# Another order for the opening of a gated linear attention and squared-ReLU kernel: the steps, loads, weight pieces and zero products of the first four blocks, and two copies on another engine

## The chip, the core and the metric

The kernel runs on one core of a Trainium2 chip. The core has a matrix engine (TensorE; PE in the profile, its weight loads PEld), three elementwise engines (VectorE or DVE, ScalarE or ACT, GpSimd or POOL), a queue from which the transfers of this kernel are issued (SyncE, SP), and 16 DMA engines that carry them out. The metric is the device time of one execution in microseconds, lower is better. Times of the old kernel: 517.73, 518.93 and 519.45 us, median 518.93.

## What is computed

Two parts follow each other. The first is a recurrence over 768 time steps for 4 batches and 8 heads of 48 channels, with a decay `alpha` for each channel; its output, turned to 3072 tokens of 384 channels, goes through two dense layers with a squared ReLU between them.

```python
# q, k, v, alpha: (4, 8, 768, 48), float32
for t in range(S):
    state = alpha[:, :, t, :, None] * state + einsum('bhd,bhe->bhde', k[:, :, t], v[:, :, t])
    y[:, :, t] = einsum('bhd,bhde->bhe', q[:, :, t], state)
x = y.transpose(0, 2, 1, 3).reshape(3072, 384)
h = maximum(x @ w_in, 0.0)          # w_in (384, 2048)
out = (h * h) @ w_out               # w_out (2048, 384)
```

The two weight matrices come to the kernel as 64-bit floats, the rest as 32-bit ones.

## The kernel before

**Tiling.** The recurrence is cut into 24 blocks, one for each batch and each stretch of 128 time steps; block n belongs to batch n % 4. Blocks 0 to 3 are the first stretch of each batch and make up the first group of 512 tokens. The dense layers work on such groups: the first layer has 16 slices of 128 hidden channels, j = 0 to 15. The weights come in 16 pieces, 8 of `w_in` and 8 of `w_out`; a piece of `w_in` serves two slices (piece 0 for j = 0 and 1, piece 1 for j = 2 and 3).

**The opening.** Everything up to the first four slices of the first group is written out by hand as a string of words, `AT['first']`. A word is the name of a step and its block (or slice, or piece). A loop reads the string from left to right and emits the instructions of each step; every engine, and the DMA queue too, gets its instructions in exactly this order. What follows (slices 4 to 15 of the first group, then groups 1 to 5) is merged from lists with due times by a planner that the change does not touch.

The words, for a block n, with the engine and the line of the profile:

- `load` (SP, L109): one transfer of 192 KB, of `a` (alpha), `q`, `k` or `v`. The string `AT['pre']` gives six loads that are issued ahead of `first`: two blocks' a, q and k. `weights` (SP, L109): a transfer of 767 KB, the next piece of weights; the number behind the word is not used, pieces come in their own order. `move` lets a transfer wait for an earlier one: it walks back over the transfers before it, adding up their assumed lengths (1.1 for a load, 2.3 for a piece), and waits for the first at which the sum has reached 2.25.
- `ln` (ScalarE, L261): logarithm of alpha. `cs` (TensorE, L283): its running sum over the 128 steps, by a product with a triangle of ones, in two passes. `ei`, `eb` (ScalarE, L298 and L294): exp of the sum with minus and plus sign. `mk`, `mq` (VectorE, L302): k and q times these.
- `qT`, `kT` (TensorE, L354): q or k turned, four transposes into one PSUM bank. `qc`, `kc` (L368): the copy of that bank into SBUF, by ScalarE or VectorE according to `AT['cp']`.
- `lt` (TensorE L337, ScalarE L344): the last row of exp, turned, and two copies of it. `sc` (TensorE, L413): scores k by q. `kv` (TensorE, L442): sums k by v, into the same two banks. `am` (VectorE, L424): masked scores. `us` (VectorE, L456), `st` (VectorE, L477 and L479): the state at the half and at the end of the block.
- `ya`, `yb` (TensorE, L393): the output y of two blocks n and n+1, in two banks, with a GpSimd instruction (L518) between the two parts. `ep` (L616): one of four parts of the copies of y into the tiles `x`; twelve copies for two blocks, each by VectorE if (n, bank, part) is in `AT['evd']`, else by ScalarE.
- `first` (ScalarE, L179) and `second` (VectorE, L192 to L199): a piece of weights made into 32-bit floats, two instructions on ScalarE, then four on VectorE.
- `ha`, `hb` (TensorE, L919; ScalarE, L925 and L928): slice j of the first layer for tokens 0 to 255 (`ha`, x of blocks 0 and 1) or 256 to 511 (`hb`, blocks 2 and 3), six products in three thirds of 128 channels each; then ReLU and square.
- `warm` (TensorE, L237) and `zeros` (TensorE, L381): products of a tile of zeros whose results nobody reads; `zeros4` stands for four products, each of which shows as two matmuls. Three `warm` products are issued ahead of the string.

What is moved and who copies is decided in two places:

```python
copy = nc.vector.tensor_copy if f"{x}{n}" in AT["cp"] else nc.scalar.copy          # copied, L368
copy = nc.vector.tensor_copy if (n, e, p) in AT["evd"] else nc.scalar.copy         # ev, L616
```

The names that the first lookup asks for are those of a letter and a block, such as 'q2'. The old list holds 'q2a', 'k2b' and the like.

Of the kernel before, what the change touches and what calls it, by code (L numbers as in the profile page):

```python
# [18 lines left out]


GB = 4
AT = {'thrp': 4.5, 'cvo': 3.35, 'thr': 2.25, 'm48': 16, 'cvs': 3.9, 'cv1': 0.125, 'later': (0, 0, 4, 6, 0, 1, 0), 'evs': 0.1, 'lead': 4, 'post': 3, 'w_first': (46.0, 38.0, 49.0), 'wstep': 1.0, 'w_in_at': 2.5, 'w_in_by': 3.6, 'room1': 22, 'room': 24, 's0': 4, 'ahead': 6, 'late': 2, 'xs': 0.0, 'g0': ((0.5, 4, False, True, 27.75), (25.75, 6, True, True), (29.25, 8, True, False)), 'sc0': (3.25, 2.35, 2.35), 'g1': ((5.5, 8, False, 15.0), (13.0, 10, True), (35.25, 12, True)), 'g': ((2.075, 6, True), (14.25, 8, True)), 'g1x': 51.0, 'gx': 48.75, 'g0x': 56.25, 'k0': 2, 'h0': 15, 'k1': 4, 'h1': 3, 'h1by': 2, 'evs0': 0.7, 'tp': 'ADMD', 'tp1': 'ADAD', 'split': 8, 'o0': (46.5, 48.5), 'o1': (), 'o2': (21.25, 24.75, 24.5, 40.0, 35.25, 28.25), 'str1': 21.5, 'ga': 9.75, 'gb': 12.5, 'cv0': -1.25, 'pre': '1a 0a 0q 0k 1k 1q', 'cp': ('q2a', 'k2b', 'k0a', 'k3a', 'k3b', 'k0b', 'q0b', 'q3b', 'q2b', 'q3a'), 'evd': ((0, 0, 0), (0, 0, 1), (0, 1, 2), (0, 1, 3), (2, 0, 3), (2, 1, 1), (2, 1, 2)), 'first': 'ln0 load1v cs0 ei0 eb0 zeros4 mk0 mq0 qT0 kT0 ln1 cs1 kc0 ei1 warm0 load0v eb1 mk1 qc0 weights0 lt1 sc0 load2a mq1 load2q kT1 kc1 qT1 load2k load3a qc1 load3k kv0 am0 first0 load3v sc1 ln2 kv1 load3q us0 am1 weights6 us1 cs2 ya0 ei2 second0 eb2 lt0 ln3 yb0 load2v mq2 qT2 mk2 load4a ep00 ep01 qc2 kT2 cs3 kc2 eb3 ei3 zeros1 sc2 ep02 mq3 mk3 kT3 ep03 weights2 first1 st0 ha0 second1 lt2 kv2 am2 qT3 load4k kc3 qc3 ha1 weights5 first2 sc3 kv3 am3 load4q us2 ha2 us3 ya2 yb2 weights3 ep20 ep21 ep22 load4v ep23 second2 first3 weights1 st1 weights4 ha3 lt3 hb0 st2 second3 hb2 hb3 hb1 st3'}


RUN = {0: 128, 32: 32, 64: 64, 96: 32}
# [3 lines left out]
def kernel(  # L29
# [78 lines left out]
    def move(us, out, in_):  # L108
        ins = nc.sync.dma_start(out=out, in_=in_).ins  # L109
        ahead = 0.0  # L110
        for before, took in reversed(under_way):
            if ahead >= AT["thrp" if us == 1.0 else "thr"]:
                tc.add_manual_dep(
# [16 lines left out]
    def load(n, xs="aqkv"):  # L130
        c, b = divmod(n, B)
        for x in xs:
            t = tile_of(x, n)
            if id(t) in owner:
                need(("free", *owner[id(t)]))
            owner[id(t)] = x, n
            given.add((x, n))
            move(
                1.1,
                out=t[:, :, 0:D] if x in "qk" else t.rearrange("a (h d) -> a h d", h=H),  # L140
                in_=srcs[x][b, :, c * C : (c + 1) * C, :].rearrange("h s d -> s h d"),
            )
# [57 lines left out]

    for word in AT["pre"].split():
        load(int(word[0]), word[1:])
# [52 lines left out]
    def work(name, bufs=1):  # L255
        return p2.tile([128, NP, C], FP32, tag=name, name=name, bufs=bufs)
# [7 lines left out]

    SPLIT = AT["split"]

# [98 lines left out]
    def copied(x, n):  # L365
        t = blk[n][f"{x}s"] = work(f"{x}s", 2 if x == "k" else 4)
        copy = nc.vector.tensor_copy if f"{x}{n}" in AT["cp"] else nc.scalar.copy
        copy(out=t, in_=blk[n].pop(f"{x}T"))  # L368
# [64 lines left out]
    def state_sums(n):  # L433
        need(("v", n), ("kb", n))
        given.add(("free", "k", n))
        ps = two[n]
        m = D if n >= AT["m48"] else 64
        for p in range(NP):
# [25 lines left out]
    def rows_of(n):  # L464
        return [slice(0, D), slice(64, 64 + D)] if n >= AT["m48"] else [slice(0, 128)]

# [712 lines left out]
```

## Time and profile before

| what | value |
|---|---|
| median of three runs | 518.93 us (517.73 to 519.45) |
| span of the profiled execution | 518.6 us |
| TensorE busy | 507.8 us, 98% |
| VectorE, ScalarE, GpSimd busy | 355.7 us, 306.4 us, 5.3 us |
| DMA, mean over the span | 197 GB/s, 102.34 MB |
| first 5 us: TensorE busy | 2.93 us |
| 15 to 20 us: TensorE, VectorE, ScalarE busy | 3.90, 4.67, 3.30 us |
| 20 to 25 us: TensorE, VectorE, ScalarE busy | 3.64, 4.83, 4.47 us |
| 40 to 60 us: TensorE busy | 20 of 20 us |

The span runs from the first to the last instruction of one execution. An engine's busy time is the sum of the times in which it carries out instructions; TensorE's ends are modelled, since its products overlap. The opening is the first 41 us or so; the stretches in the table show where in it TensorE stands still.

### The profile page before, as it was taken

To read this page: it belongs to the slowest core of one execution; us is meant where nothing else is said; L and a number is where in the kernel's file an instruction comes from. 1 tells how busy PE (TensorE), PEld (TensorE's weight loads), DVE (VectorE), ACT (ScalarE), POOL (GpSimd) and SP (SyncE) were. 2 spreads that over 40 slices of the span, in tenths; PEclk is the share of its full clock that TensorE was granted. 3 is DMA by queue.
4 is the path that set the end of the run, shared out by engine and by line. 5 is a ranking of instruction groups with operands and counts; after the bars stand their busy time and mean duration, and the time that the engine had idled before them with its cause. 6 is when DMAs were issued, how large, how long until landed. Compare 5 with 4: busy or idle time off the path is not lost.

```text
span 518.6 us, 13019 instructions
## 1 busy us (share of the span) xinstructions
PE 507.8 (98%) x5338; PEld 418.9 (81%) x5338; DVE 355.7 (69%) x628; ACT 306.4 (59%) x649; POOL 5.3 (1%) x29
## 2 busy tenths in 40 slices
PE   7899999999999999999999999999999999999997
PEld 5675455678888669987899988899988899988997
DVE  2766669986887877776697468587465487363861
ACT  4788898547888653485664276772275673164620
POOL 4000000000000000000000000000000000000000
PEclk9999999999999999999999999999999999999999
DMA  9999779472777786898884688864683545699201
GB/s 183 204 267 237 197 189 235 93 228 80 238 190 184 246 243 162 265 279 227 205 225 143 222 247 222 223 200 152 213 274 124 185 121 154 207 380 322 65 2 61
DMA packets 139323, 102.34 MB, mean 197 GB/s; under 512 B 109808, under 2 KB 115968, under 8 KB 139264
## 3 DMA queue, kind: packets, MB, share of 16 engines
q1 hardware_dynamic: 139264, 101.51, 68.2%
q8 instruction: 42, 0.69, 0.6%
q14 instruction: 17, 0.14, 0.1%
HBM read 84.16 MB, written 17.33 MB: 196 GB/s over the span
## 4 chain that ended last, share of the span: by engine, by line
PE 93%; DVE 4%; issue 1%; POOL 1%; ACT 1%; DVEq 0%; POOLq 0%
PE o L809 39%; PE h L726 32%; PE h L919 8%; PE y L393 4%; PE sckv L413 2%; PE T L578 2%; PE sckv L442 2%; PE cs L283 1%; PE cs L286 1%; DVE x L616 1%; PE cs L287 1%; DVE hd L648 1%; DVE hx L653 0%; DVE am L424 0%; ACT x L616 0%
## 5 line engine op out<-in xcount | busy, mean ns | idle before, releaser
L726 PE MATMUL h<-xd,wd 128*128 128x512 f32 x240 | 68.1, 396 | 1.1 <-issue 1.1
L726 PE MATMUL h<-xa,wb 128*128 128x512 f32 x240 | 68.7, 394 | 0.0
L726 PE MATMUL h<-xl,wl 128*128 128x512 f32 x240 | 67.9, 391 | 0.0
L648 DVE TENSOR_TENSOR hid<-h,hid 128x512 f32<-128x512 f32 x40 | 27.6, 689 | 51.1 <-PE h L726 51.0
L616 ACT COPY x<-y 48x256 f32<-48x256 f32 (+3 forms) x133 | 46.7, 365 | 21.2 <-PE y L393 18.8
L809 PE MATMUL o<-wb,ha 128*128 128x384 f32 x160 | 54.5, 340 | 0.0
L743 ACT ACTIVATE h<-h 128x512 f32<-128x512 f32 x40 | 23.3, 582 | 52.3 <-PE h L726 52.3
L809 PE MATMUL o<-wl,hl 128*128 128x384 f32 x160 | 53.7, 336 | 0.1
L809 PE MATMUL o<-wd,hd 128*128 128x384 f32 x304 | 53.7, 334 | 0.0
L809 PE MATMUL o<-w_out,hid 128*128 128x384 f32 x160 | 53.6, 489 | 0.0
L726 PEld LDWEIGHTS h<-xl,wl 128*128 128x128 f32 x240 | 45.1, 188 | 10.1 <-DVE xl L653 0.4
L809 PEld LDWEIGHTS o<-wd,hd 128*128 128x128 f32 x304 | 52.8, 188 | 0.0
L726 PEld LDWEIGHTS h<-xa,wb 128*128 128x128 f32 x240 | 44.4, 188 | 9.8 <-ACT hid L763 0.4
L726 PEld LDWEIGHTS h<-xd,wd 128*128 128x128 f32 x240 | 44.0, 188 | 9.1
L809 PE MATMUL o<-wb,hx 128*128 128x384 f32 x144 | 48.3, 336 | 0.0
L809 PE MATMUL o<-wl,hx 128*128 128x384 f32 x144 | 48.1, 334 | 0.0
L809 PEld LDWEIGHTS o<-w_out,hid 128*128 128x128 f32 x160 | 30.0, 190 | 19.7
L741 ACT ACTIVATE hid<-h 128x512 f32<-128x512 f32 x40 | 24.2, 606 | 32.9 <-PE h L726 32.5
L919 PE MATMUL h<-x,w_in 128*128 128x512 f32 (+1 forms) x120 | 43.4, 512 | 0.2 <-DVE x L616 0.2
L701 ACT ACTIVATE ha<-hid 128x512 fp32r<-128x512 f32 x40 | 25.1, 642 | 20.3 <-PE o L809 7.9
L919 PEld LDWEIGHTS h<-x,w_in 128*128 128x128 f32 x120 | 22.1, 190 | 17.8 <-issue 15.3
L653 DVE SCALAR_TENSOR_TENSOR hl<-ha,hid 128x512 fp32r<-128x512 f32 x40 | 27.5, 687 | 6.9 <-ACT ha L701 6.8
(111 smaller groups left out, 852.5 us busy)
## 6 DMA issues: line engine op xcount, KB each, us to landing
wd<-do SPq DMA_DIRECT2D x36, 384.0 KB
wl<-lo SPq DMA_DIRECT2D x34, 384.0 KB
wl<-li SPq DMA_DIRECT2D x32, 384.0 KB
wd<-di SPq DMA_DIRECT2D x32, 384.0 KB
raw<-in_moe_w_out_dram SPq DMA_DIRECT2D x8, 767.5 KB
raw<-in_moe_w_in_dram SPq DMA_DIRECT2D x8, 767.2 KB
v_in<-in_v_dram SPq DMA_DIRECT2D x24, 192.0 KB
out_dram<-osb SPq DMA_DIRECT2D x24, 192.0 KB
```

The lines of the kernel that those rows point to most:

```text
L393: ins = nc.tensor.matmul(out=ys[e][64 * half : 64 * half + D + G * e, m % 2, p // 2, t], lhsT=lhsT, rhs=rhs, start=(half, e) not in seen, ...
L413: nc.tensor.matmul(out=ps[e][HALF[h], 0, p, :], lhsT=ks[rows, p, HALF[h]], rhs=qs[rows, p, HALF[h]], start=True, stop=True, skip_group_che ...
L442: nc.tensor.matmul(out=ps[h][64 * e : 64 * e + m, 1, p, G:64], lhsT=tile_of("k", n)[HALF[h], 2 * p + e, 0:m], rhs=tiles["v"][n % NV][HALF[ ...
L616: copy(out=x[kk][to : to + m, t : t + 2], in_=blk[n]["y"][e][r : r + m, :, p // 2],)
L648: nc.vector.tensor_tensor(out=o, in0=x, in1=z, op=op)
L653: nc.vector.scalar_tensor_tensor(out=o, in0=x, scalar=c, in1=y, op0=ALU.mult, op1=op)
L701: nc.scalar.activation(out=a, in_=x, func=AF.Copy, scale=NEAR * E)
L726: nc.tensor.matmul(out=acc["h", j], lhsT=here[w, "i", p][:, kk, jj * 128 : (jj + 1) * 128], rhs=x_parts[x][:, kk], start=start and kk == 0 ...
L741: nc.scalar.activation(out=hid[j], in_=x, func=AF.Copy, scale=E)
L743: nc.scalar.activation(out=x, in_=x, func=AF.Copy, scale=1.0 + E)
L809: nc.tensor.matmul(out=acc[t][:, 0:DM], lhsT=lhs[:, t * C : (t + 1) * C], rhs=rhs, start=start, stop=stop, skip_group_check=True,)
L919: nc.tensor.matmul(out=ps, lhsT=w[:, kk, c0 : c0 + 128], rhs=xT[g][kk][:, cols], start=(kk == 0), stop=(kk == KM - 1),)
```

## The change

Only the table `AT` changes, in five entries. The order of the six first loads is different (a0 comes third in place of second). The list `cp` names q1 and q2, which moves the copies `qc1` and `qc2` from ScalarE to VectorE. The list `evd` has eight entries in place of seven: for blocks 0 and 1 VectorE copies parts 1 and 3 of both banks (before: parts 0 and 1 of bank 0, 2 and 3 of bank 1); for blocks 2 and 3 all four parts of bank 0 (before: part 3 of bank 0, parts 1 and 2 of bank 1). The string `first` holds the same steps in another order; it has the same 14 loads, 7 pieces of weights, 4 conversions and 8 half slices as before. The zero products are seven in six places in place of five in two.

```diff
-'pre': '1a 0a 0q 0k 1k 1q'
+'pre': '1a 0q 0a 1k 0k 1q'
-'cp': ('q2a', 'k2b', 'k0a', 'k3a', 'k3b', 'k0b', 'q0b', 'q3b', 'q2b', 'q3a')
+'cp': ('q1', 'q2')
-'evd': ((0, 0, 0), (0, 0, 1), (0, 1, 2), (0, 1, 3), (2, 0, 3), (2, 1, 1), (2, 1, 2))
+'evd': ((0, 0, 1), (0, 0, 3), (0, 1, 1), (0, 1, 3), (2, 0, 0), (2, 0, 1), (2, 0, 2), (2, 0, 3))
-'first': 'ln0 load1v cs0 ei0 eb0 zeros4 mk0 mq0 qT0 kT0 ln1 cs1 kc0 ei1 warm0 load0v eb1 mk1 qc0
-  weights0 lt1 sc0 load2a mq1 load2q kT1 kc1 qT1 load2k load3a qc1 load3k kv0 am0 first0 load3v sc1
-  ln2 kv1 load3q us0 am1 weights6 us1 cs2 ya0 ei2 second0 eb2 lt0 ln3 yb0 load2v mq2 qT2 mk2 load4a
-  ep00 ep01 qc2 kT2 cs3 kc2 eb3 ei3 zeros1 sc2 ep02 mq3 mk3 kT3 ep03 weights2 first1 st0 ha0 second1
-  lt2 kv2 am2 qT3 load4k kc3 qc3 ha1 weights5 first2 sc3 kv3 am3 load4q us2 ha2 us3 ya2 yb2 weights3
-  ep20 ep21 ep22 load4v ep23 second2 first3 weights1 st1 weights4 ha3 lt3 hb0 st2 second3 hb2 hb3
-  hb1 st3'
+'first': 'ln0 warm0 ln1 load0v cs0 eb0 mq0 weights3 zeros1 ei0 mk0 qT0 qc0 cs1 ei1 eb1 zeros1 mk1
+  zeros1 load1v kT0 kc0 mq1 zeros1 load2a kT1 load2k sc0 load3a kc1 qT1 kv0 lt1 qc1 am0 load2q load3q
+  us0 first0 lt0 sc1 kv1 am1 zeros2 ln2 cs2 us1 weights6 eb2 ya0 yb0 ei2 second0 mk2 ln3 load3k ep00
+  mq2 weights5 load3v load2v cs3 weights1 ep01 eb3 qT2 mq3 zeros1 qc2 kT2 ep02 ei3 kc2 qT3 ep03 sc2
+  first1 mk3 qc3 ha0 kT3 kc3 first2 load4k ha1 weights4 sc3 kv3 lt3 st0 am2 second1 kv2 load4a am3
+  us2 ha2 us3 ya2 lt2 yb2 ep20 ep21 ep22 weights0 ep23 second2 st1 ha3 st3 hb1 hb0 load4v st2 first3
+  second3 hb3 load4q hb2 weights2'
```

More of the change, by code (lines that the diff above doesn't have):

```diff
@@ L21 @@
 GB = 4
-AT = {'thrp': 4.5, 'cvo': 3.35, 'thr': 2.25, 'm48': 16, 'cvs': 3.9, 'cv1': 0.125, 'later': (0, 0, 4, 6, 0, 1, 0), 'evs': 0.1, 'lead': 4, 'post': 3, 'w_first': (46.0, 38.0, 49.0), 'wstep': 1.0, 'w_in_at': 2.5, 'w_in_by': 3.6, 'room1': 22, 'room': 24, 's0': 4, 'ahead': 6, 'late': 2, 'xs': 0.0, 'g0': ((0.5, 4, False, True, 27.75), (25.75, 6, True, True), (29.25, 8, True, False)), 'sc0': (3.25, 2.35, 2.35), 'g1': ((5.5, 8, False, 15.0), (13.0, 10, True), (35.25, 12, True)), 'g': ((2.075, 6, True), (14.25, 8, True)), 'g1x': 51.0, 'gx': 48.75, 'g0x': 56.25, 'k0': 2, 'h0': 15, 'k1': 4, 'h1': 3, 'h1by': 2, 'evs0': 0.7, 'tp': 'ADMD', 'tp1': 'ADAD', 'split': 8, 'o0': (46.5, 48.5), 'o1': (), 'o2': (21.25, 24.75, 24.5, 40.0, 35.25, 28.25), 'str1': 21.5, 'ga': 9.75, 'gb': 12.5, 'cv0': -1.25, 'pre': '1a 0a 0q 0k 1k 1q', 'cp': ('q2a', 'k2b', 'k0a', 'k3a', 'k3b', 'k0b', 'q0b', 'q3b', 'q2b', 'q3a'), 'evd': ((0, 0, 0), (0, 0, 1), (0, 1, 2), (0, 1, 3), (2, 0, 3), (2, 1, 1), (2, 1, 2)), 'first': 'ln0 load1v cs0 ei0 eb0 zeros4 mk0 mq0 qT0 kT0 ln1 cs1 kc0 ei1 warm0 load0v eb1 mk1 qc0 weights0 lt1 sc0 load2a mq1 load2q kT1 kc1 qT1 load2k load3a qc1 load3k kv0 am0 first0 load3v sc1 ln2 kv1 load3q us0 am1 weights6 us1 cs2 ya0 ei2 second0 eb2 lt0 ln3 yb0 load2v mq2 qT2 mk2 load4a ep00 ep01 qc2 kT2 cs3 kc2 eb3 ei3 zeros1 sc2 ep02 mq3 mk3 kT3 ep03 weights2 first1 st0 ha0 second1 lt2 kv2 am2 qT3 load4k kc3 qc3 ha1 weights5 first2 sc3 kv3 am3 load4q us2 ha2 us3 ya2 yb2 weights3 ep20 ep21 ep22 load4v ep23 second2 first3 weights1 st1 weights4 ha3 lt3 hb0 st2 second3 hb2 hb3 hb1 st3'}
@@ new lines @@
+AT = {'thrp': 4.5, 'cvo': 3.35, 'thr': 2.25, 'm48': 16, 'cvs': 3.9, 'cv1': 0.125, 'later': (0, 0, 4, 6, 0, 1, 0), 'evs': 0.1, 'lead': 4, 'post': 3, 'w_first': (46.0, 38.0, 49.0), 'wstep': 1.0, 'w_in_at': 2.5, 'w_in_by': 3.6, 'room1': 22, 'room': 24, 's0': 4, 'ahead': 6, 'late': 2, 'xs': 0.0, 'g0': ((0.5, 4, False, True, 27.75), (25.75, 6, True, True), (29.25, 8, True, False)), 'sc0': (3.25, 2.35, 2.35), 'g1': ((5.5, 8, False, 15.0), (13.0, 10, True), (35.25, 12, True)), 'g': ((2.075, 6, True), (14.25, 8, True)), 'g1x': 51.0, 'gx': 48.75, 'g0x': 56.25, 'k0': 2, 'h0': 15, 'k1': 4, 'h1': 3, 'h1by': 2, 'evs0': 0.7, 'tp': 'ADMD', 'tp1': 'ADAD', 'split': 8, 'o0': (46.5, 48.5), 'o1': (), 'o2': (21.25, 24.75, 24.5, 40.0, 35.25, 28.25), 'str1': 21.5, 'ga': 9.75, 'gb': 12.5, 'cv0': -1.25, 'pre': '1a 0q 0a 1k 0k 1q', 'cp': ('q1', 'q2'), 'evd': ((0, 0, 1), (0, 0, 3), (0, 1, 1), (0, 1, 3), (2, 0, 0), (2, 0, 1), (2, 0, 2), (2, 0, 3)), 'first': 'ln0 warm0 ln1 load0v cs0 eb0 mq0 weights3 zeros1 ei0 mk0 qT0 qc0 cs1 ei1 eb1 zeros1 mk1 zeros1 load1v kT0 kc0 mq1 zeros1 load2a kT1 load2k sc0 load3a kc1 qT1 kv0 lt1 qc1 am0 load2q load3q us0 first0 lt0 sc1 kv1 am1 zeros2 ln2 cs2 us1 weights6 eb2 ya0 yb0 ei2 second0 mk2 ln3 load3k ep00 mq2 weights5 load3v load2v cs3 weights1 ep01 eb3 qT2 mq3 zeros1 qc2 kT2 ep02 ei3 kc2 qT3 ep03 sc2 first1 mk3 qc3 ha0 kT3 kc3 first2 load4k ha1 weights4 sc3 kv3 lt3 st0 am2 second1 kv2 load4a am3 us2 ha2 us3 ya2 lt2 yb2 ep20 ep21 ep22 weights0 ep23 second2 st1 ha3 st3 hb1 hb0 load4v st2 first3 second3 hb3 load4q hb2 weights2'}
```

## The prediction

> **What bounds the kernel now.** I read the page first, then the waits of TensorE, then the timelines of TensorE, ScalarE, VectorE and the DMA queue over the first 45 us. The columns of a timeline line are start, length, engine, line, operation, tiles, count, and in brackets the idle time before it with its releaser.
>
> ```profile
> span 518.6 us, 13019 instructions
> PE 507.8 (98%) x5338; PEld 418.9 (81%) x5338; DVE 355.7 (69%) x628; ACT 306.4 (59%) x649; POOL 5.3 (1%) x29
> ...
> PE cs L283 <- POOL us L226: 1.6, 1, 1.6
> PE h L726 <- issue: 1.1, 1, 1.1
> PE warm L237 <- POOL s L70: 1.1, 1, 1.1
> PE cs L283 <- ACT a_lent L261: 1.1, 1, 1.1
> PE kT L354 <- DVE qk_lent L302: 0.9, 1, 0.9
> PE lastT L337 <- ACT b L294: 0.5, 1, 0.5
> PE qT L354 <- DVE qk_lent L302: 0.4, 1, 0.4
> PE h L919 <- DVE x L616: 0.2, 1, 0.2
> ```
>
> TensorE is the bound. Of its waits all but the 1.1 us at L726 lie in the opening, and together they are 5.8 us (1.6+1.1+1.1+0.9+0.5+0.4+0.2). The last is at 37.04 us:
>
> ```profile
> 36.10 0.88 DVE L616 COPY x<-y 32x256 f32<-32x256 f32 x2 [0.21 <-ACT x L616]
> 37.04 8.45 PE L919 MATMUL h<-x,w_in 128*128 128x256 f32 x29 [0.21 <-DVE x L616]
> ```
>
> There the third third of a first-layer half product (an hb step) takes up the x that VectorE finished at 36.98. From there on TensorE does not stop, and the steps left are the same in both orders: 20 products of 256 columns at 0.216 us, then the planned part. So the change is worth what it moves this one moment, as long as nothing behind it runs dry. I therefore carry the new order forward to the same moment and compare with 37.04.
>
> **The stages, from the rows.** The rows that the working uses most:
>
> ```profile
> 5.67 1.62 PE L283 MATMUL cs<-a_in,causal_r 128*128 128x384 f32 x2 [1.64 <-POOL us L226]
> 7.08 1.92 PE L381 MATMUL zeros<-s 128*128 128x128 f32 x8
> 8.93 1.11 PE L354 MATMUL qT<-ident,q_in 128*128 128x128 f32 x4
> 9.83 0.68 PE L354 MATMUL kT<-ident,k_in 128*128 128x128 f32 x4
> ...
> 17.25 0.91 PE L283 MATMUL cs<-a_lent,causal_r 128*128 128x384 f32 x2 [1.06 <-ACT a_lent L261]
> ...
> 5.04 0.60 SPq L109 DMA_DIRECT2D q_in<-in_q_dram  x1
> 6.20 1.63 SPq L109 DMA_DIRECT2D v_in<-in_v_dram  x2
> ```
>
> cs0 is put down to GpSimd, but ln0 on ScalarE ended at 5.56 (5.04+0.52), and that is the real releaser. The issues at 5.04 and 6.20 each waited for the landing of the load four places ahead (a0, then q0), so a place on the queue is 1.16 us.
>
> *First sums.* a0 goes from second to third place: cs0 starts at 5.67+1.16 = 6.83. It still runs at the slow rate (1.62 to its end, 8.45). ScalarE's exp of it takes 0.49 (8.97), mq0 0.55 (9.55), qT0 starts at 9.66, against 8.93: **+0.7**. One pair of zero products lies in that gap, where before there were four pairs.
>
> *Blocks 0 and 1.* From then on I go by start-to-start times of TensorE steps in the same trace: turn 0.47, cs 0.65, a zero pair 0.22, scores 0.53, state sums 0.54, last row (lt) 0.46. qT0 to 10.29 (part of it slow), cs1 10.94, two zero pairs 11.38, kT0 11.85, zero pair 12.07. kT1 waits for VectorE: cs1 is out at 11.10, exp 11.64, mk1 12.23, so kT1 at 12.37, sc0 12.84, qT1 13.37, kv0 13.87, lt1 14.41, lt0 14.87, sc1 15.33, kv1 15.86, against 15.56: **+0.3**. Of 0.46 us of this, lt0 is work that stood at 19.18 before. The added zero products here cost nothing: they lie ahead of kT1, which waits anyway; without that cover the three pairs would cost 0.66. qc1 on VectorE (about 0.5, from the 0.47 of a 128x384 product and ScalarE's 0.48 for the same copy) ends ahead of am0, which waits for kv0 in any case.
>
> *Block 2's logarithm.* ScalarE works in the order of the list, and ln2 stands behind the first half of a weight piece (two ACTIVATEs, 1.90) and now also behind lt0's copies (0.32). lt1's copies end at 15.3, first0 at 17.2, lt0's copies 17.5, ln2 18.04, cs2 18.10, against 17.25: **+0.85**, the largest loss.
>
> *Opening products of y.* cs2 0.84, us part 0.49, am part 0.80 up to yb0, since lt0 no longer covers the hand-over by GpSimd (0.61 with that cover, 0.80 without it, as at 33.02): yb0 20.23, against 19.64: **+0.6**.
>
> *Blocks 2 and 3 turned.* am1 and us1 end at 17.53, second0 takes 2.85, mk2 0.47, mq2 ends 21.40; qT2 21.54 (20.73 before), but cs3 (0.65) now stands ahead of it, inside the wait. VectorE then makes three of the x copies (0.455 each, from 21.75, when ScalarE has left the same bank) and mq3 by 23.66; qT3 23.8. On ScalarE three copies, eb3, three copies, ei3, kc2: 24.65. sc2 24.71, ha0 25.24, against 24.82: **+0.4**. The second copy given to VectorE, qc2, is off ScalarE, which is the later of the two here: on ScalarE it would make this +0.9.
>
> *To the end of yb2.* TensorE is unbroken in both. Before, ha0 to ha3 is 33.65-24.82 = 8.83. After: lt3 (0.46) has moved in ahead of yb2, qT3 and kT3 change places, and lt2 now covers the hand-over (-0.2): 9.05. ha3 34.29, **+0.64**, of which 0.46 is work done early.
>
> *The x copies of blocks 2 and 3.* Before, seven on ScalarE and five on VectorE alternate in the same two banks: the row at 36.10 waited for a copy of ScalarE, and the last ends 3.23 after yb2 (33.75). After, VectorE has all six of one bank and ScalarE all six of the other: 0.1+6x0.455 = 2.8, **-0.4**. yb2 ends 34.4, the last copy 37.2, TensorE goes on at 37.35.
>
> **Sum:** 37.35-37.04 = **+0.3 us**. The same way of carrying forward, tried on the old order, comes out 0.3 late at 37.04, so the sum may be 0.7 too high (-0.4); where rows had to be chosen, the slower ones add 0.5. Its bounds: -0.4 to +0.8. The profiled execution is 518.6 by its span and the median of the runs 518.93, so I add the difference to the median: **519.2**, 518.5 to 519.7.
>
> Cover behind the moment: second3 ends near 44.7 (44.23 before), and its piece is first used at 47.25; ScalarE's first3 stands behind two more products, but TensorE met no full PSUM there before. If that cover were gone, each us would count in full.
>
> **Loads.** v3 and v2 move behind two weight pieces. From the landing of a0 to that of k4 (5.04 to 30.8, where the issue of the next q waited for it) there are 16 loads and three pieces; after, from q0 in that place to v2, 14 loads and three pieces, two loads less at 1.05 (the six from 5.04 to 11.19 took 1.03 each): 28.7, and v3 27.6. kv3 wants v3 at 29.0 and kv2 wants v2 at 30.0: 1.3 us to spare.
>
> **Rivals.** *The fast rate comes late (slower).* The four turns from 8.93 take 1.11 us and start 0.21 apart, the four from 9.83 0.68, the last of them 0.11 apart, as all later ones: TensorE's rate doubles at 9.98, though the granted clock is printed as full throughout. It came after 4.31 us of unbroken work (5.67 to 9.98); 2.93 us of it (1.10 to 4.03) had not been enough. After, work is broken between 8.66 and 9.66. If it must start anew there, the fast rate comes at 9.66+4.31 = 13.97. Four us at half rate lose 2.0, less the 0.3 that kT1 waits: +1.7, **520.9**. It decides if a break of 1.0 us counts; against it, breaks of 1.06 and 0.86 at 17.25 and 24.35 did not take the rate away again. [...]
>
> *The fast rate comes early (faster).* warm0 moves to the front: four warm products are 3.8 us unbroken (1.10 to 4.88), between the 2.93 that were too few and the 4.31 that were enough. Then cs0, its zero pair and qT0 are fast, 0.95 less up to cs1, and nothing later takes it back, since the first weight piece lands near 14 and first0 then starts at 14.3: +0.3-0.95, **518.3**; with the lower bound of the sum 517.6. Against it: the gap of two us that follows.
>
> *v3 or v2 land late (slower).* If loads and pieces, mixed otherwise, take 2.3 us more than that count, v2 lands at 31.0 against 30.0, and all that stands behind kv2 on TensorE waits: +1, **520.2**; a further us for each further us of the queue. For it: the queue is already the fullest resource here after TensorE, and a third piece now stands ahead of v3 and v2.
>
> *The copies do not move as said.* The old list holds names like 'q2a', which the lookup of 'q2' never meets: all eight copies are on ScalarE. The new list moves q1 and q2 alone, no k. If they did nothing, sc2 would come 0.5 later: **519.7**.
>
> **Chances.** The sum as worked 0.46, late rate 0.22, early rate 0.18, late loads 0.09, copies of no effect 0.05. 0.3% is about 1.55 us, what a measurement of this kernel can tell from no change: slower means over 520.5, faster under 517.4. Slower: most of the late rate, half of the late loads and the tail of the sum, 0.28. Faster: the early rate together with the low end of the sum, and gains in the six stages that I rounded up, 0.20. Within: 0.52. Range 516.9 to 521.2, wide enough for both rates of TensorE.
>
> **What would show it.** cs0 near 6.8, qT0 near 9.7, cs2 near 18.1, sc2 near 24.7, ha0 near 25.2, the wait of h L919 for x near 37.3. The spacing of the turns and of cs1 tells which rate they run at. Wrong would be: waits for v_in or raw ahead of sckv L442; x copies that still alternate; any wait of TensorE after 38 us, which would mean that the planned part did not take the shift on as it is.

## The result and the profile after

The changed kernel takes 521.70 us (median of five runs, 520.63 to 523.26) against 519.23 us for the old one beside it (five runs, 517.73 to 519.45): a ratio of 1.0056 (95% interval 1.0039 to 1.0074). It is slower by about 2.5 us, and outside the predicted range.

The profiled execution is the fastest of those five, 520.63 us with a span of 518.8 us. So its trace has to be read with care: it shows almost none of the loss. First the head of its page, with the span and the busy times.

```profile
span 518.8 us, 13034 instructions
...
PE 506.8 (98%) x5342; PEld 418.5 (81%) x5342; DVE 357.3 (69%) x631; ACT 305.4 (59%) x646; POOL 5.3 (1%) x29
```

Then TensorE's waits in the same execution (total us, times, longest).

```profile
PE h L726 <- issue: 1.7, 1, 1.7
PE cs L283 <- ACT a_in L261: 1.5, 1, 1.5
PE cs L283 <- ACT a_lent L261: 1.2, 1, 1.2
PE warm L237 <- POOL s L70: 1.1, 1, 1.1
PE qT L354 <- DVE q_in L302: 1.0, 1, 1.0
...
```

And the steps that the prediction followed, from the timelines of TensorE, ScalarE and VectorE of this execution (start, length, engine, line, operation, count, idle time before it).

```profile
6.39 0.88 PE L283 MATMUL cs<-a_in,causal_r 128*128 128x384 f32 x2 [1.52 <-ACT a_in L261]
7.11 0.38 PE L381 MATMUL zeros<-s 128*128 128x128 f32 x2
8.45 0.66 PE L354 MATMUL qT<-ident,q_in 128*128 128x128 f32 x4 [0.95 <-DVE q_in L302]
...
17.20 0.91 PE L283 MATMUL cs<-a_lent,causal_r 128*128 128x384 f32 x2 [1.20 <-ACT a_lent L261]
...
33.61 2.29 ACT L616 COPY x<-y 32x256 f32<-32x256 f32 x6 [0.31 <-PE y L393]
34.01 2.67 DVE L616 COPY x<-y 48x256 f32<-48x256 f32 x6 [3.12 <-ACT x L616]
36.73 9.73 PE L919 MATMUL h<-x,w_in 128*128 128x256 f32 x32 [0.21 <-DVE x L616]
46.30 0.81 PE L283 MATMUL cs<-a_in,causal_r 128*128 128x384 f32 x2
```

The last of these steps in the old kernel's trace:

```profile
46.61 0.81 PE L283 MATMUL cs<-a_in,causal_r 128*128 128x384 f32 x2
```

What to see there: cs0 takes 0.88 us, not the 1.62 of the old trace, and the four turns 0.66, not 1.11. TensorE ran at its full rate from before cs0 on; the trace has it granted at 5.58. The moment at which it takes up x after the opening is 36.73, 0.31 *earlier* than the old 37.04. The first sums of block 4, the first step behind it that both orders have, are 46.30 against 46.61. The 0.3 us are then more than given back at L726, in a wait that no semaphore explains (1.74 us against 1.11).

This gives a way to account for every trace. The start of the first sums of block 4, plus 470.85 us, plus TensorE's waits put down to "issue" behind that point, is the span of both kernels to 0.1 us: old 46.61+470.85+1.11 = 518.57, profiled 518.6; changed 46.30+470.85+1.74 = 518.89, profiled 518.8. It holds to 0.15 us in fifteen of the twenty traces of this study, to 0.4 us in two; the three that miss it by 1.9 to 2.7 us have small products added, and lose more behind that point than these waits, as shown below. So a trace of these two orders loses time in the opening or in waits of that kind.

### The profile page after: what moved, and what is told of

The parts are those of the page before. It is cut to its first block, busy times and chain, and to the rows that moved or that the text cites. A ratio compares the mean times of both kernels' runs of the same rounds, so it can differ in the third digit from the quotient of the medians.

```text
span 518.8 us, 13034 instructions
## 1 busy us (share of the span) xinstructions
PE 506.8 (98%) x5342; PEld 418.5 (81%) x5342; DVE 357.3 (69%) x631; ACT 305.4 (59%) x646; POOL 5.3 (1%) x29
## 4 chain that ended last, share of the span: by engine, by line
PE 93%; DVE 4%; issue 1%; DMA 1%; ACT 1%; SPq 0%; DVEq 0%; POOLq 0%
PE o L809 39%; PE h L726 32%; PE h L919 8%; PE y L393 4%; PE sckv L413 2%; PE T L578 2%; PE sckv L442 2%; PE cs L283 1%; DVE x L616 1%; DMA a_in<-in_alpha_dram 1%; PE cs L286 1%; PE cs L287 1%; DVE hd L648 1%; DVE hx L653 0%; DVE am L424 0%
## 5 line engine op out<-in xcount | busy, mean ns | idle before, releaser
L726 PE MATMUL h<-xa,wb 128*128 128x512 f32 x240 | 68.9, 394 | 1.7 <-issue 1.7
L726 PE MATMUL h<-xd,wd 128*128 128x512 f32 x240 | 68.0, 396 | 0.0
L726 PE MATMUL h<-xl,wl 128*128 128x512 f32 x240 | 67.9, 391 | 0.0
L616 ACT COPY x<-y 32x256 f32<-32x256 f32 (+1 forms) x132 | 46.4, 365 | 19.5 <-PE y L393 17.5
L726 PEld LDWEIGHTS h<-xl,wl 128*128 128x128 f32 x240 | 45.1, 188 | 11.9 <-issue 1.9
L726 PEld LDWEIGHTS h<-xa,wb 128*128 128x128 f32 x240 | 44.4, 188 | 9.8 <-ACT hid L763 0.4
L726 PEld LDWEIGHTS h<-xd,wd 128*128 128x128 f32 x240 | 44.1, 188 | 9.1
```

The lines of the kernel that those rows point to most:

```text
L616: copy(out=x[kk][to : to + m, t : t + 2], in_=blk[n]["y"][e][r : r + m, :, p // 2],)
L726: nc.tensor.matmul(out=acc["h", j], lhsT=here[w, "i", p][:, kk, jj * 128 : (jj + 1) * 128], rhs=x_parts[x][:, kk], start=start and kk == 0 ...
```

## The experiments

**First question: what does a typical execution of the changed kernel look like?** Both kernels were run again, unedited. The theory then was that the longer wait at L726 made the loss (theory S); its rival was that the fast rate comes late or goes away again in most executions.

Old kernel again (no edit):

> The old kernel against itself, for the spread of one kernel and for a second trace. Every theory expects a ratio of 1.000 with an interval that holds 1. What it tells apart is where executions differ: if by TensorE's rate in the opening (theory rate), the moment at which TensorE takes up x after the opening (37.04 in the first trace) moves by up to 2 us between traces and all behind it moves along; if by the wait of TensorE for nothing shown near 238 us (theory stall, 1.1 us in the first trace), that moment stays within 0.3 us and the wait changes.

519.71 us (12 runs), ratio 1.0005 [0.9985, 1.0024]. Its trace takes up x at 36.94 and waits 0.2 us at "issue".

Changed kernel again (no edit):

> The changed kernel again: ratio 1.004 to 1.007. Theory rate: a trace of a typical execution has the fast rate of TensorE only after some 13 us, not at 5.6 as in the first trace, and takes up x near 38.5 in place of 36.73. Theory stall: x is taken up near 36.7 and the wait near 237 us is 2.5 us or more, in place of 1.74.

522.01 us (12 runs, 520.88 to 523.35), ratio 1.0041 [1.0026, 1.0056]. The profiled execution took 523.10 us, more than the median, and its trace has the loss in full, span 521.3 us. Its timeline of TensorE:

```profile
6.59 0.88 PE L283 MATMUL cs<-a_in,causal_r 128*128 128x384 f32 x2 [1.72 <-ACT a_in L261]
7.31 0.38 PE L381 MATMUL zeros<-s 128*128 128x128 f32 x2
8.65 1.12 PE L354 MATMUL qT<-ident,q_in 128*128 128x128 f32 x4 [0.95 <-DVE q_in L302]
9.56 1.49 PE L283 MATMUL cs<-a_in,causal_r 128*128 128x384 f32 x2
...
18.64 1.65 PE L283 MATMUL cs<-a_lent,causal_r 128*128 128x384 f32 x2 [1.20 <-ACT a_lent L261]
...
39.71 2.64 PE L919 MATMUL h<-x,w_in 128*128 128x256 f32 x11 [0.21 <-DVE x L616]
```

The same steps in the same order, but qT0, cs1 and cs2 take twice as long: the rate was there at cs0 (0.88) and gone at qT0 (1.12). The windows of the same trace, cut where the granted clock changes (busy us and count of each engine in the order PE, PEld, DVE, ACT, POOL; then the granted clock, the DMA share, GB/s):

```profile
4.93:8.35 3.42, 1.10 (x4) 0.68 (x4) 0.31 (x1) 1.77 (x4) 1.26 (x6) 1.00 1.39 181
8.35:11.76 3.41, 3.11 (x11) 2.51 (x12) 0.87 (x3) 1.30 (x4) 0.00 (x0) 0.50 1.15 292
11.76:15.17 3.41, 3.39 (x93) 2.87 (x93) 1.72 (x4) 1.37 (x3) 0.00 (x0) 1.00 1.08 210
15.17:18.59 3.42, 2.27 (x94) 2.01 (x90) 2.57 (x8) 3.04 (x7) 0.00 (x0) 1.00 0.96 211
18.59:22.00 3.41, 3.36 (x66) 2.28 (x66) 2.82 (x5) 1.28 (x3) 0.00 (x0) 0.50 0.98 284
```

In this trace the rate changes at 4.93, 8.35, 11.76, 18.59 and 22.00, points that lie 3.41 us or twice that apart. After a stretch in which TensorE was busy 1.10 of 3.42 us it falls to half; after one with 3.11 of 3.41 us it comes back; after the stretch with the gap ahead of cs2, busy 2.27 of 3.42 us, it falls again. x is taken up 2.98 us later than in the changed kernel's first trace; 0.2 us of this is cs0, which starts later, and some 1.4 us are left for each lost stretch. The wait at L726 is 1.08 us here, no longer than in the old kernel. Theory S falls.

Compare the old kernel's windows around the same place, from its trace before the change:

```profile
3.15:6.57 3.42, 1.78 (x5) 0.79 (x4) 0.00 (x0) 0.52 (x1) 2.78 (x12) 1.00 1.05 192
6.57:9.98 3.41, 3.41 (x15) 2.88 (x14) 1.03 (x2) 1.28 (x3) 0.00 (x0) 1.00 1.42 187
```

The printed clock is 1.00 here only because nothing is recorded ahead of the first grant, at 9.98; the durations show half rate (cs0 1.62 us, 0.88 in the trace above). What matters is the second line: cs0, four zero products and the first turns leave no gap, and the stretch is full (3.41 of 3.41 us). The gap ahead of cs0 is as long in the old order (1.64 us) as in two traces of the new one (1.5 and 1.7). The difference is what lies behind it: in the new order one zero product is left, TensorE waits 0.95 us more ahead of qT0, and with the rate granted by then the little work in between takes about half the time (cs0 0.88 us). The stretch from 4.93 to 8.35 above, which covers most of both gaps, holds 1.10 us.

In that trace the old kernel was at half rate, so like with like is its second one, where the rate is granted at 3.97:

```profile
5.54 0.88 PE L283 MATMUL cs<-a_in,causal_r 128*128 128x384 f32 x2 [1.51 <-ACT a_in L261]
6.26 1.05 PE L381 MATMUL zeros<-s 128*128 128x128 f32 x8
8.45 0.66 PE L354 MATMUL qT<-ident,q_in 128*128 128x128 f32 x4 [1.14 <-DVE q_in L302]
```

Both gaps are there too. But the zero products between them take 1.05 us, against 0.38 in the new order; the stretch from 3.97 to 7.38 holds 1.83 us of work, and the rate stays.

A third trace of the changed kernel, from a single run:

> One more trace of the changed kernel. Theory rate: whichever way the stretches fall, x is taken up later than 37.0 us in as much as TensorE's rows show half rate between 5 and 22 us: 3.4 us at half rate cost about 1.5 us; without any, 36.7.

522.28 us, span 520.5. The rate is granted at 4.38 and lost at 7.80 for 6.8 us; x is taken up at 39.54. Its windows:

```profile
4.38:7.80 3.42, 1.30 (x6) 0.68 (x4) 0.00 (x0) 1.00 (x3) 1.69 (x8) 1.00 1.31 194
7.80:14.62 6.82, 5.87 (x38) 4.82 (x40) 2.06 (x4) 3.18 (x7) 0.00 (x0) 0.50 1.05 234
```

The first grants in the traces lie between 3.92 and 14.03 us, so the stretches counted from them lie differently against the kernel's start in each execution. Two of the three traces of the changed kernel have the loss and one has not, so a single trace misled; that the place of the stretches decides it is the author's inference. Two of the 12 runs above print a granted clock of 1.000 and yet took 522.01 and 523.35 us. They may have been granted the rate late and not have lost it, since the printed clock leaves out the time ahead of the first grant; no trace of the changed kernel shows such a run.

**Second question: which part of the change loses the rate?** First, parts undone or done alone.

The old order of the first six loads in the changed kernel:

```diff
-'pre': '1a 0q 0a 1k 0k 1q'
+'pre': '1a 0a 0q 0k 1k 1q'
```

> The changed kernel with the old order of the six first loads: a0 lands 1.2 us earlier, and the first sums start near 5.6. Theory rate: the break of TensorE ahead of the first sums shrinks from 1.5 us to 0.7 or less, the fast rate comes early in more executions, and of the 0.56% at least half is gone: ratio 1.000 to 1.003. Theory stall: the instructions of TensorE are the same, ratio 1.004 to 1.007.

520.79 us (12), ratio 1.0012 [0.9989, 1.0034]. By the ratio most of the loss is gone, but the interval overlaps that of the changed kernel, and the runs lie far apart, 517.91 to 522.57 us. The profiled execution lost the rate twice, at 7.33 and 17.57, with first sums of block 4 at 48.21, although its cs0 came at 5.42, 1 us earlier than in the changed kernel. Four executions took less than 519.2 us, at a clock of 0.999 or 1.000; that they kept the rate from early on is likely, but no trace shows it.

The new copies alone, in the old kernel:

```diff
-'cp': ('q2a', 'k2b', 'k0a', 'k3a', 'k3b', 'k0b', 'q0b', 'q3b', 'q2b', 'q3a')
+'cp': ('q1', 'q2')
-'evd': ((0, 0, 0), (0, 0, 1), (0, 1, 2), (0, 1, 3), (2, 0, 3), (2, 1, 1), (2, 1, 2))
+'evd': ((0, 0, 1), (0, 0, 3), (0, 1, 1), (0, 1, 3), (2, 0, 0), (2, 0, 1), (2, 0, 2), (2, 0, 3))
```

> The old kernel with the new lists cp and evd alone. Both theories: the last copy of x ends 0.3 to 0.5 us earlier and nothing else changes, ratio 0.999 to 1.000. If the copies carry the loss (a third theory, unlikely by the trace), 1.004 or more.

520.26 us (12), ratio 1.0007 [0.9991, 1.0022]; the last x copy ends at 37.01 against 36.98. The copies are no part of the loss, but the gain expected of them did not come either. The waits of its TensorE say why:

```profile
PE sckv L413 <- DVE qs L368: 1.6, 2, 1.3
```

In the old order VectorE has other work when q is turned, so a copy given to it makes the scores wait up to 1.3 us.

The changed kernel without its seven zero products (their results are read by nobody):

```diff
-weights3 zeros1 ei0 ... eb1 zeros1 mk1 zeros1 load1v ... mq1 zeros1 load2a ... am1 zeros2 ln2 ... mq3 zeros1 qc2
+weights3 ei0 ... eb1 mk1 load1v ... mq1 load2a ... am1 ln2 ... mq3 qc2
```

> The changed order without its seven zero products. Theory rate lost: emptier stretches, the full rate is lost in more executions and comes late in more, ratio 1.006 to 1.010. Theory order: the products are taken out of time in which TensorE mostly waits, ratio 1.002 to 1.004.

522.28 us (6), ratio 1.0053 [1.0035, 1.0072]. As they are placed, the seven do nothing that the time shows. All six runs have a clock of 0.984 to 0.997, so all lost the rate, against 6 of the 12 of the changed kernel at 0.997 or less; fewer instructions also move the wait at "issue" (0.3 us at y L393 in this trace, none at L726; more below), so the two effects are not told apart. In the trace the rate was first granted at 12.81 and lost from 19.64 to 23.05.

The old kernel with its four zero products moved, same instructions, from behind cs0 to behind the warm product:

```diff
-eb0 zeros4 mk0 ... warm0 load0v
+eb0 mk0 ... warm0 zeros4 load0v
```

> The old kernel with its four zero products moved from behind cs0 (7.1 to 8.9 us, where TensorE would wait) to behind warm0. Same instructions. Theory rate: the old kernel now has the changed one's trouble, the full rate comes at 12 us or later or is lost near 8, ratio 1.003 to 1.007. Theory order: four products of 0.22 us move into a gap of 0.5 us, ratio 1.000 to 1.001.

520.84 us (12), ratio 1.0033 [1.0016, 1.0050]: most of the loss, made in the old kernel by that one move. Its timeline of TensorE at the place they left:

```profile
5.21 0.88 PE L283 MATMUL cs<-a_in,causal_r 128*128 128x384 f32 x2 [1.19 <-ACT a_in L261]
8.56 1.12 PE L354 MATMUL qT<-ident,q_in 128*128 128x128 f32 x4 [2.47 <-DVE q_in L302]
```

A gap of 2.47 us lies between them, and the rate, granted at 4.73, is gone from 8.14 to 11.56. The first sums of block 4 are 1.0 us later than in the old trace (47.61 against 46.61). So the four zero products behind cs0 were not idle filling: with them there the old kernel's second trace kept the rate, without them this one lost it.

**Third question: if the gaps are filled in the new order, is the loss gone?** The first attempt used more of the same zero products: three more behind the warm product, three behind cs0, four ahead of cs2, ten in all (the expectation counts eleven).

```diff
-warm0 ln1 ... weights3 zeros1 ei0 ... am1 zeros2 ln2
+warm0 zeros3 ln1 ... weights3 zeros4 ei0 ... am1 zeros6 ln2
```

> The changed order with eleven zero products in its two early and one late gap of TensorE (three behind warm0, three more behind cs0, four more ahead of cs2), all in time in which TensorE waits anyway. Theory rate lost (TensorE falls back to half rate after a stretch of 3.4 us with too little in it, and gets the full rate back a stretch later): no stretch at 0.50 is left after the rate has been granted, x is taken up near 36.8, ratio 0.998 to 1.001 against the old kernel where the changed order has 1.004. Theory order (the new order is slower in itself, by its waits): the ten products add work, ratio 1.004 to 1.006.

525.07 us (6), ratio 1.0096 [1.0073, 1.0118]. Only the first two places (six products more):

> Only the two early gaps filled (three behind warm0, three more behind cs0). Theory rate lost: the half-rate stretch near 8.4 to 11.8 is gone, the one near 18.6 to 22 stays in some executions; about half of the loss is gone, ratio 1.001 to 1.003. Theory order: 1.004 to 1.005.

525.68 us (6), ratio 1.0117 [1.0089, 1.0145]. Only the third place (four more):

> Only the late gap filled (six products in place of two ahead of cs2). Theory rate lost: the half-rate stretch near 18.6 is gone, the one near 8.4 stays in some executions; ratio 1.001 to 1.003. Theory order: 1.004 to 1.005.

531.48 us (5), ratio 1.0218 [1.0193, 1.0244]. All three are slower still, against what was expected, and for another reason: in the trace of the six early ones x is taken up at 37.11, so the opening is healthy, and the time is lost hundreds of microseconds later. The waits of TensorE with four more products, and two places of its timeline:

```profile
PE y L393 <- issue: 7.2, 3, 3.2
```

```profile
35.79 0.24 PE L393 MATMUL y<-am,v_in 64*48 64x64 f32 x2
39.24 0.27 PE L393 MATMUL y<-am,v_in 64*64 64x64 f32 x1 [3.21 <-issue]
...
244.46 0.33 PE L393 MATMUL y<-am,v_in 64*48 64x64 f32 x3 [2.93 <-issue]
```

TensorE stops 2.93 and 3.21 us in the middle of a row of short products, with no releaser that the profile shows, and after both stops the rate is lost for 3.4 us more (40.12 to 43.53, 244.91 to 248.33). The page's list of DMA queues (kind, packets, MB, share of 16 engines; here of the changed kernel) has a queue whose packets come just ahead of these waits:

```profile
q8 instruction: 42, 0.69, 0.5%
```

0.69 MB in 42 packets is 16.4 KB each. TensorE has 2x5342 = 10,684 matmuls and weight loads, with its 162 semaphore and drain instructions 10,846. All of these counted through each trace, as the number that stands ahead of the wait, with the large packets of q8 beside them:

```
kernel        instructions ahead          packet of q8      wait ends   length
old            5569                       236.8 to 237.7    239.08      1.11
changed        5569                       235.7 to 236.6    238.00      1.74
changed again  5569                       238.0 to 239.0    240.35      1.08
four more      1218                        36.7 to  37.6     39.24      3.21
               5569                       242.2 to 243.2    244.46      2.93
               8129                       345.7 to 346.7    348.30      1.02
```

A wait stands at the same count, 5569, in all four traces, with either order and with the four products added; the three counts are whole multiples of 256 apart to within one (4351 = 17x256-1, 2560 = 10x256), and each wait ends 1.3 to 1.6 us after a packet has come. What TensorE waits for there is not shown; that it is its next instructions is the author's inference from these counts and packets. Instructions added ahead move other work to that count: with eight matmuls and their eight weight loads more, it falls into a burst of short products (32 of them in 0.7 us, where L726 has three in 0.84), and the wait at 5569 is 2.93 us there, against 1.08 to 1.74 at L726.

The next attempt fills the gaps and keeps the count of instructions. A step was added that makes one zero product of n x 128 columns in place of n:

```diff
+def wide(n):
+    ps = bank(n, "wide", (4, 128))
+    nc.tensor.matmul(out=ps[:, 0:n, :], lhsT=zeros_128x128, rhs=zeros_broadcast_128xnx128, ...)
-warm0 ln1 ... weights3 zeros1 ei0 ... eb1 zeros1 mk1 ... am1 zeros2 ln2
+warm0 wide2 ln1 ... weights3 wide3 ei0 ... eb1 mk1 ... am1 wide4 wide3 ln2
```

> The changed order with as many instructions on TensorE as it has, but longer zero products in its gaps: one of the seven moves behind warm0 and has 256 columns, the one behind cs0 has 384, the two ahead of cs2 have 512 and 384, in place of 128 each. Two theories are apart now. Theory rate: TensorE gets its full rate late or loses it, and the longer products keep it; no waits of the kind issue above 2 us, ratio 0.997 to 1.001. Theory order: the gaps and their order cost the time whatever the rate does, ratio 1.003 to 1.006. [...]

520.14 us (12), ratio 1.0016 [1.0003, 1.0030], between what the two theories had expected. In the trace the rate is granted only at 10.00 and then kept, and x is taken up at 37.93. Only the first two places, that is the product ahead of cs0 (256 columns, taken from between eb1 and mk1) and the one behind cs0 (384 columns):

```diff
-warm0 ln1 ... weights3 zeros1 ei0 ... eb1 zeros1 mk1
+warm0 wide2 ln1 ... weights3 wide3 ei0 ... eb1 mk1
```

> Only the two early products are longer. Theory rate: what is lost before 12 us is gained back, the loss near 18.6 stays in some executions, ratio 0.999 to 1.003. Theory order: 1.003 to 1.006.

519.63 us (11, 519.20 to 520.93), ratio 1.0001 [0.9992, 1.0009]. The loss is gone; the granted clock was at least 0.999 in all 11 runs, where the trace of the moved zero products, which lost the rate for 3.42 us, prints 0.997; so none lost it for that long once it had been granted. The opening in its timeline (lines of the file stand eight lower):

```profile
4.67 0.71 PE L389 MATMUL wide<-s 128*128 128x256 f32 x2
6.61 0.88 PE L283 MATMUL cs<-a_in,causal_r 128*128 128x384 f32 x2 [1.23 <-ACT a_in L261]
7.33 0.81 PE L389 MATMUL wide<-s 128*128 128x384 f32 x2
8.67 0.66 PE L354 MATMUL qT<-ident,q_in 128*128 128x128 f32 x4 [0.53 <-DVE q_in L302]
```

cs0 and qT0 start when they do in the changed kernel's trace with the loss (6.59 and 8.65); what differs is the zero products ahead of cs0 and behind it, and the turns take 0.66 in place of 1.12. Nothing on the other engines was touched, and the number of TensorE's instructions is the same. Together with the moved products of the old kernel, this run settles the cause.

Only the gap ahead of cs2:

```diff
-am1 zeros2 ln2
+am1 wide4 wide3 ln2
```

> Only the two products ahead of cs2 are longer. Theory rate: the late grant and the early loss stay, ratio 1.002 to 1.004. Theory order: 1.003 to 1.006.

521.50 us (6), ratio 1.0032 [1.0020, 1.0044]. It does little: in the trace the rate was lost for 6.8 us from 7.65. But it fills the same gap as the four added small products, with no instruction more, and takes 10 us less: the instructions, not the time in the gap, made those so slow.

Each early place by itself, first the product behind cs0, then the one ahead of it:

```diff
-weights3 zeros1 ei0
+weights3 wide3 ei0
```

> The changed order with only the product behind cs0 longer (384 columns in place of 128). If the loss comes from the emptier stretch behind the first sums, where the old order has four products and the new one has one, this alone gives most of it back: ratio 0.999 to 1.002. If it comes from the gap ahead of the first sums, which the later a0 makes longer, 1.003 to 1.005.

```diff
-warm0 ln1 ... eb1 zeros1 mk1
+warm0 wide2 ln1 ... eb1 mk1
```

> The changed order with only one product moved into the gap ahead of the first sums (256 columns). If the gap ahead is what counts: ratio 0.999 to 1.002; if the stretch behind the first sums: 1.002 to 1.005.

520.71 and 520.78 us (12 each), both with ratio 1.0027 (to 1.0046 and 1.0042). Either may take away a part of the loss, though the intervals reach into that of the changed kernel; only both together bring the ratio to 1. The two traces show the other way to lose time: the rate is granted late, at 10.09 and 14.03, and then kept, and x is taken up at 37.95 and 38.77.

**Fourth question: with the rate kept, is the new order worth anything?** The two early products together with the old order of the loads, which has cs0 a microsecond earlier:

```diff
-'pre': '1a 0q 0a 1k 0k 1q'
+'pre': '1a 0a 0q 0k 1k 1q'
-warm0 ln1 ... weights3 zeros1 ei0 ... eb1 zeros1 mk1
+warm0 wide2 ln1 ... weights3 wide3 ei0 ... eb1 mk1
```

> Both early products longer and the old order of the six first loads, so that a0 lands 1.2 us earlier. The rate is kept and the first sums start near 5.5; what stands behind is bound by ScalarE and VectorE, so 0.3 to 1 us of it is left at the end: ratio 0.997 to 1.000, at best a little better than both kernels.

519.70 us (11), ratio 1.0002 [0.9986, 1.0018]. The profiled execution has the first sums of block 4 at 45.48, 1.1 us ahead of the old trace, the earliest of all, and a span of 517.46; but 4 of the 11 runs have a granted clock of 0.992 to 0.996, and the ratio missed the 0.997 to 1.000 that was expected. The gap ahead of cs2 filled as well:

```diff
-am1 zeros2 ln2
+am1 wide3 wide2 ln2
```

> The changed order with the old order of the six first loads, both early products longer and the two ahead of cs2 with 384 and 256 columns in place of 128 each. Theory rate: no half-rate stretch is left after the first grant in nearly all executions, x is taken up near 36.0, ratio 0.996 to 0.999: faster than both. If the slow executions of the kernel with the two early products alone had another cause, 1.000 as that one.

519.40 us (12), ratio 0.9992 [0.9976, 1.0007], the clock at least 0.999 in all 12: the rate is kept, but the gain that was expected of it is not seen. And the old kernel with two of its four zero products made 256 columns wide, one of them ahead of cs0:

```diff
-ln0 load1v ... eb0 zeros4 mk0
+ln0 wide2 load1v ... eb0 wide2 zeros2 mk0
```

> The old order with one of its four zero products behind cs0 moved, with 256 columns, into its gap ahead of cs0, and another made 256 wide to keep the time behind cs0. Theory rate: the few executions of the old kernel that lose the rate (some 12%) go away and more get it early, ratio 0.997 to 1.000. Theory order: 1.000.

519.11 us (12), ratio 0.9983 [0.9967, 1.0000]. The ratio is as expected, but the loss of the rate did not go away: three of the 12 have a clock of 0.993 to 0.997, and the profiled one, 521.09 us, lost the rate from 18.57 to 25.40 and took up x at 39.02. No version is clearly faster than the old kernel. The new order with the rate kept is its equal. What single traces gain in the opening, up to 1.1 us, does not show in the medians; the waits at "issue" differ by more than that from trace to trace (0 to 1.7 us in kernels with no small products added), but what takes the gain back is not settled.

## Why the prediction was wrong

**What held.** TensorE bounds the kernel, the change is worth what it moves one moment, and the planned part takes the shift on, but for the waits at "issue". The carried-forward sum was +0.3 us with bounds of -0.4 and +0.8. Measured with the rate kept from 5.58 on it is -0.31 (36.73 against 37.04); in the trace with the wide product behind cs0, where the rate came at 10.09, near the 9.98 that the sum took over from the old order, it is +0.91 (x at 37.95, first sums of block 4 at 47.52), just over the upper bound. The sum lies between. That it is near is in part luck: in the second of these traces, whose rate is nearest to its premise, qT0 comes earlier than said (9.20 for 9.66) and cs2 and ha0 later (18.31 for 18.10, 25.56 for 25.24). The copies went as read from the lookups: VectorE has all six of one bank, ScalarE all six of the other. Loads were on time; none of the three traces of the changed kernel has TensorE waiting for v ahead of L442 or ScalarE for raw weights ahead of 37 us.

**Terms that were mis-sized.** In the changed kernel's first trace the stages came earlier than said: qT0 8.45 for 9.66, cs2 17.20 for 18.10, ha0 24.45 for 25.24, ha3 33.48 for 34.29. The reason is the rate, there from 5.58, where the sum had half rate up to 9.66; the "largest loss", +0.85 at cs2, is -0.05 in this trace and +1.39 in the one that loses the rate (18.64 against 17.25). The place of a0 on the queue was about right: cs0 starts at 6.39, 6.59 and 6.81 in three traces of the new order and at 5.54 and 5.67 in two of the old, 1.0 us for the 1.16 predicted. The x copies were to gain 0.4 and gain 0.14: from ScalarE's first copy to VectorE's last it takes 3.07 us (33.61 to 36.68), before 3.21 (33.77 to 36.98). VectorE's six start 0.40 after ScalarE's, behind its first copy, although each engine has a bank of its own, and this wait was in the working at 0.1.

**The step that failed** is the dismissal of the rival that the rate comes late: "It decides if a break of 1.0 us counts; against it, breaks of 1.06 and 0.86 at 17.25 and 24.35 did not take the rate away again." The two breaks of the old trace stood in stretches that were otherwise filled (2.68 to 2.97 us of 3.41, by its windows counted on from 9.98), and from them nothing follows for a stretch that holds a good part of a break of 1.7 or 2.1 us ahead of cs0 and most of another of 0.95 behind it. The length of one break does not tell the traces apart. The two that lost the rate lost it behind stretches that held 1.10 and 1.30 us of 3.42 (windows above). The rival, with a chance of 0.22, named the right place and the right resource, but in another form: it has the rate come late, while in the two traces with the loss it came early and was taken away again. It was also too cheap: 520.9 is 4.3 us at half rate, less a wait that hides 0.3. The two traces with the loss have two stretches, or one of double length, and take up x 2.5 and 2.7 us later than the old trace (39.54 and 39.71 against 37.04).

Beside it stands an assumption that was never put as a step: that "the added zero products here cost nothing", and so that those taken away behind cs0 cost nothing either. The four of the old order were counted as filling of a gap, one pair against four, in the sentence on the first sums; what they did for the rate was not asked. Moving them, alone, made the ratio 1.0033.

In the traces shown here the rate comes and goes at points 3.41 us apart, or multiples of that, and the first grants are scattered between 3.92 and 14.03 us. In the opening it fell back with no break of TensorE longer than 2.47 us, the one that the moved zero products left; a thin stretch was enough there.

**The other rivals.** The early rate did come, at 3.9 to 5.7 us in ten of the fifteen traces of the new order, but not for the reason of its rival, the fourth warm product: with only three in a row the old order has it too, at 3.97 in its second trace, at 4.21 with the new copies and at 4.73 with the zero products moved. In that second trace the rate came within the same 2.93 us of work (1.10 to 4.03) that "had not been enough" in the first, so the length of that work alone does not decide it. It is also worth little to the old order, where x is taken up at 36.94 with the rate from 3.97 and at 37.04 with it from 9.98. In the new order it is then mostly lost again in the gaps around cs0, the first of which was named against it, so an execution that gains at cs0 pays later. Late v2 and v3 fell; copies of no effect fell.

**What stays open.** How much a stretch has to hold for the rate to stay. A stretch with 1.66 of 3.42 us busy (5.58 to 9.00 in the changed kernel's first trace) kept the rate, one with 1.65 (3.92 to 7.33, with the old load order) lost it, and one with 2.27, mostly in short or narrow products (15.17 to 18.59 above), lost it too. Busy time as printed is not the whole measure. That short products count for less does not settle it either: the old kernel's second trace kept the rate over 14.21 to 17.63 with 1.72 us, 0.70 of it in wide products, while the stretch with 2.27 has 0.71 of it in products of 128 columns. What the waits at "issue" wait for was inferred from counts and packets, and from the run with wide products; it was not shown.

## What to carry to other kernels

Zero products that nobody reads can be doing work: here the move of four of them, alone, made the ratio 1.0033. So before moving or dropping one, look at how full it leaves TensorE around its gaps; in this kernel stretches of 3.42 us with 1.10 and 1.30 us of work were followed by half rate, and a full one (3.41 of 3.41 us) by the full rate. One profiled execution can be the lucky one; compare its time to the median before explaining the difference with it, and profile again when it lies at the edge. Where a gap has to be filled, fill it with few long products: here four short ones more added waits of up to 3.21 us elsewhere, and the ratio was 1.0218, against 1.0032 with long ones in the same gap.

## What was not expected of the hardware

- In the changed kernel's second trace TensorE's rate fell back to half after a stretch of 3.42 us in which it was busy 1.10 us, with no break longer than 1.72 us, and returned after a stretch of 3.41 us with 3.11 us; the two lost stretches of that trace cost some 2.8 us. A granted clock of 0.993, as in that run, also stands in 13 of the 138 runs of the unedited old kernel that were taken with the experiments.
- The mean granted clock leaves out the time ahead of the first grant: the old trace, granted at 9.98, prints 1.00 while cs0, at 5.67, takes 1.62 us in place of 0.88.
- Turns (transposes) follow the rate like products: four took 1.12 us at half rate and 0.66 us at full, cs0 1.62 and 0.88.
- TensorE stopped at the same count of its instructions, 5569, in four traces, and in one of them also at 1218 and 8129, which lie 17x256-1 and 10x256 away: 1.08 to 1.74 us in the traces of both kernels, up to 3.21 us inside a burst of short products. Four added zero products, 16 instructions, brought the ratio to 1.0218; the same gap filled with no instruction more, 1.0032.
- With a PSUM bank for each of the two copying engines the second still began behind the first one's first copy, 0.40 us late.
